# First blocks, moments and V weights reordered at the head of an attention kernel

## The chip, the core and the metric

The kernel runs on one core of a Trainium2 chip. The metric is the device time of one execution in microseconds (us). Before the change three runs gave 1567.88, 1568.05 and 1568.91, median 1568.05. One more execution was recorded by the profiler: it took 1567.75, of which the profile's span is 1566.0.

The engines are called as the profile calls them: PE is TensorE (PEld its weight loads), DVE VectorE, ACT ScalarE, POOL GpSimd, SP SyncE, which here only issues DMAs. "SPq", "ACTq" and "POOLq" are an engine's instructions that issue DMAs.

## The reference

```python
B, S, D, H, F = 1, 2048, 512, 32, 1376         # heads of 16
xn = (x - mean(x)) / sqrt(var(x) + 1e-5)        # over D
q, k, v = split(xn @ wqkv)                      # D x 3D
p = softmax(q @ k.T * 16 ** -0.5)               # per head, 2048 x 2048
s = (p @ v) @ wo
g = silu(gelu(xn @ w1 + b1) @ w2 + b2)          # D x F, F x D
out = x + s * g                                 # everything float32
```

## The kernel before

The 2048 tokens are 16 blocks (t) of 128 and 4 chunks (c) of 512, so a chunk is four blocks. Every large product of the first half is made of three matmuls on rounded halves: an operand is split in a high part (rounded to the matmul's type by a copy on ACT) and a low part (operand minus high part, on DVE or POOL), and the terms are high·high, low·high and high·low. `mm3` (L81) issues the three for one slice of the contraction.

The order of all instructions is written out by hand; each engine runs its own in that order and waits on semaphores for what it reads. DMAs stand in the queue of the engine that issues them, in the order of issue. Three parts follow each other: the root (to about 45 us), where xn, its transposes and the first q, k and V come about; the MLP with the remaining q and k and the maxima of the scores (to about 478 us); and the attention loop with the projection behind it. The change lies in the root alone.

The root, by its helpers:

- `load_x` (L402) loads a block of x, 256 KB. Blocks 1 and 3 are on ACT's queue, the others on SP's, in this order: x 0, x 2, the q and k weights of two groups, x 4 and 5, four pieces of V's weights (`wv_r`). Each further block takes the buffer of the one six before it (XB = 6), once that one's norm has read it.
- `moments` (L411, L412): bn_stats and bn_aggr of one block on DVE, into mv.
- `rstd` (L416 to L421) for four blocks at once: add eps (DVE), square root (ACT), reciprocal and three DVE steps that refine it (a Newton step). All are 128x4 elements.
- `norm` (L425): one 128x512 pass of DVE per block into xn; then the load of the block six later is issued.
- `ln(t, n)`: moments of n blocks, one rstd, n norms.
- `turn` (L434): four PE transposes of a block, then `split` of the result in xh and xl: high copy on ACT (L75), low part on DVE (L76).
- `pool_after` (L492): a one-element POOL operation that reads xn of a block, and so parks POOL until that block's norm is done.
- V's weights: high copies on ACT (L503), low parts on POOL (`wv_low`, L495), four pieces k each, in the space of a later kt tile (the profile calls them kt).
- the q and k weights of the first two groups: high on ACT (L289), low on POOL (L290).
- `q_first(c)` (L450): 24 matmuls for one chunk, three terms by two groups by four k. `evac` takes the result out: ACT copies both groups from PSUM (hg, L365), rounds both (hh, L369), POOL makes the low parts (hl, L370), and SP stores both to DRAM (qk_h L375, qk_l L376).
- `v_tile(t)` (L81): 12 matmuls of a V block, and `v_out`.
- `load_first`: after q_first(1), twelve gathers on SP's queue (L124 and L142) that read chunk 0's and chunk 1's q and k back from DRAM in another layout (gt), for the first score matmuls (L190).
- `consts`: on POOL, a memset, the DMA of ones, a cast of the identity, and the DMAs of b1 and b2.

PE's order in the root is: 22 dummy matmuls on the identity, transposes of blocks 0 to 3, q_first(0), transposes of 4 to 7, v_tile(0), q_first(1), transposes of 8 to 11, v_tile(1), q_first(2), transposes of 12 to 15, then the pairs of the MLP and the score part, where the first L190 read gt.

ACT's order is the square root of blocks 0 to 3, the weights' high copies, the four L75 of blocks 0 to 3, four L503, the square root of 4 to 7, hg and hh of chunk 0, the L75 of 4 to 7, and so on. POOL's is `pool_after(3)`, two L290, three L495, consts, `pool_after(7)`, the fourth L495, hl of chunk 0, and so on.

Of the kernel before, what the change touches and what calls it, by code (L numbers as in the profile page):

```python
# [8 lines left out]
F32 = mybir.dt.float32  # L9
F32R = mybir.dt.float32r  # L10
AF = mybir.ActivationFunctionType
# [5 lines left out]
P = 128  # L17
# [32 lines left out]
def fused(ctx: ExitStack, tc: tile.TileContext, x, wqk, wv, wo, w1, b1, w2, b2, out):  # L50
# [307 lines left out]

    def evac(us, ph):
        raws = [wk.tile([P, CH], F32, name="hg", bufs=2) for u in us]  # L360
        for u, raw in zip(us, raws):
            if u[0] == "m":
                nc.scalar.activation(raw, ph.pop(u), AF.Gelu_apprx_tanh, bias=b1_sb[:, u[2]:u[2] + 1])
            else:
                nc.scalar.activation(raw, ph.pop(u), AF.Copy)  # L365
        for u, raw in zip(us, raws):
            hh = wk.tile([P, CH], F32R, name="hh", bufs=HB)
# [16 lines left out]
    with ExitStack() as s1:  # L384
# [14 lines left out]
        def load_x(t):  # L399
            xs[t] = w1k.tile([P, D], F32, name="xt", bufs=XB)  # L400
            eng = nc.scalar if t in (1, 3) else nc.sync
            eng.dma_start(xs[t], x[t * P:(t + 1) * P, :])  # L402
# [3 lines left out]
        mv = wp.tile([P, NT, 2], F32, name="mv")  # L406
        ve = wp.tile([P, 5, NT], F32, name="ve")

        def moments(t):
            st = w1k.tile([P, 6], F32, name="st")  # L410
            nc.vector.bn_stats(st, xs[t])  # L411
            nc.vector.bn_aggr(mv[:, t, :], st)  # L412

        def rstd(t0, t1):
            v = ve[:, :, t0:t1]
            nc.vector.tensor_scalar(v[:, 0], mv[:, t0:t1, 1], EPS, None, op0=OP.add)  # L416
            nc.scalar.activation(v[:, 1], v[:, 0], AF.Sqrt)
            nc.vector.reciprocal(v[:, 2], v[:, 1])
            nc.vector.scalar_tensor_tensor(v[:, 3], v[:, 2], -0.5, v[:, 2], op0=OP.mult, op1=OP.mult)
            nc.vector.tensor_mul(v[:, 3], v[:, 3], v[:, 0])  # L420
            nc.vector.scalar_tensor_tensor(v[:, 4], v[:, 3], 1.5, v[:, 2], op0=OP.add, op1=OP.mult)  # L421

        def norm(t):
            xns[t] = w1k.tile([P, D], F32, name="xn", bufs=4)
            nc.vector.tensor_scalar(xns[t], xs.pop(t), mv[:, t, 0:1], ve[:, 4, t:t + 1],  # L425
                                    op0=OP.subtract, op1=OP.mult)
            if t + XB < NT:
                load_x(t + XB)
# [9 lines left out]
        def v_tile(t):  # L438
            pv = a_tile((P, D))
            c, ts = t // NCH, slice(t % NCH * P, t % NCH * P + P)  # L440
            for k in range(KT):
                mm3(pv, (xh[c][:, k, ts], xl[c][:, k, ts]), (wv_h[:, k], wv_l[:, k]), k == 0, k == KT - 1)
            v_out(t, pv)

        def q_first(c):
            pq = {("q", g, c): a_tile((P, CH)) for g in range(2)}
            for n, (i, j) in enumerate(((0, 0), (1, 0), (0, 1))):
                for g in range(2):
                    for k in range(KT):
                        nc.tensor.matmul(pq["q", g, c], W1[g][i][:, k * P:(k + 1) * P], (xh, xl)[j][c][:, k],  # L450
                                         start=n == 0 and k == 0, stop=n == 2 and k == KT - 1)
            evac(list(pq), pq)

        for t in range(4):
            load_x(t)
        warm = wp.tile([1, 2], F32, name="warm")
        nc.vector.memset(warm, 1.0)
        nc.scalar.activation(warm[:, 1:], warm[:, :1], AF.Sqrt)
        for g in range(2):
# [11 lines left out]
        def consts():  # L471
# [4 lines left out]
            nc.gpsimd.tensor_copy(ident_r, ident)  # L476
            nc.gpsimd.dma_start(b1_sb, b1)
            nc.gpsimd.dma_start(b2_sb, b2.rearrange("(o d) -> o d", o=1).to_broadcast([P, D]))

        pw = ps_v.tile([P, D], F32, name="pv")  # L480
        for _ in range(22):
            nc.tensor.matmul(pw[:, :P], ident, ident, start=True, stop=True)
        def ln(t, n):
            for i in range(t, t + n):
                moments(i)
            rstd(t, t + n)
            for i in range(t, t + n):
                norm(i)
# [9 lines left out]
        for g in range(2):  # L498
            W1[g] = w_split(W1[g], "w1", 4)
        for t in range(NCH):  # L500
            turn(t)
        for k in range(KT):
            nc.scalar.activation(wv_h[:, k], wv_r[:, k], AF.Copy)  # L503
        for k in range(KT - 1):
            wv_low(k)
        ln(NCH, NCH)
        consts()
        pool_after(2 * NCH - 1)
        wv_low(KT - 1)
        q_first(0)  # L510
        for c in range(1, NCH):
            for t in range(NCH * c, NCH * c + NCH):
                turn(t)
            if c < NCH - 1:
                ln(NCH * c + NCH, NCH)
            else:
                nc.scalar.activation(warm[:, 1:], warm[:, :1], AF.Gelu_apprx_tanh)
                w1_load(0)
                w2_load(0)
                w2_load(1)  # L520
                break
            v_tile(c - 1)
            q_first(c)
            if c == 1:
                load_first()

    keep_r = ctx.enter_context(tc.tile_pool(name="keep_r", bufs=1, side="right"))
# [521 lines left out]
```

## Time and profile before

| what | value |
|---|---|
| median of three runs | 1568.05 us |
| profiled execution | 1567.75 us |
| its span | 1566.0 us |
| PE busy | 1555.4 us (99%) |
| DVE busy | 1390.1 us (89%) |
| ACT busy | 1244.4 us (79%) |
| POOL busy | 375.4 us (24%) |
| PE busy, 0 to 9.73 / 9.73 to 19.45 / 19.45 to 42 us | 6.92 / 7.88 / 22.55 us |
| granted PE clock | 1.00 in every window |

Times in the profile run from the span's start. A line of a timeline has the start, the length from the first start to the last end of a group, the engine, the line of the kernel, the operation, what it writes and reads (partitions by elements), the count, and in brackets how long the engine had stood idle before and what ended that. Matmuls overlap, so the pitch of a row of them is taken from start to start. A line of the chain of waits has start, length and work; it is followed back from the last instruction of the window to what released each. A DMA's time from issue to landing is longer than its issue instruction.

### The profile page before, as it was taken

To read this page: it belongs to the slowest core of one execution; us is meant where nothing else is said; L and a number is where in the kernel's file an instruction comes from. 1 tells how busy PE (TensorE), PEld (TensorE's weight loads), DVE (VectorE), ACT (ScalarE), POOL (GpSimd) and SP (SyncE) were. 2 spreads that over 40 slices of the span, in tenths; PEclk is the share of its full clock that TensorE was granted. 3 is DMA by queue.
4 is the path that set the end of the run, shared out by engine and by line. 5 is a ranking of instruction groups with operands and counts; after the bars stand their busy time and mean duration, and the time that the engine had idled before them with its cause. 6 is when DMAs were issued, how large, how long until landed. Compare 5 with 4: busy or idle time off the path is not lost.

```text
span 1566.0 us, 32580 instructions
## 1 busy us (share of the span) xinstructions
PE 1555.4 (99%) x12254; PEld 955.0 (61%) x12254; DVE 1390.1 (89%) x2306; ACT 1244.4 (79%) x2487; POOL 375.4 (24%) x392
## 2 busy tenths in 40 slices
PE   8999999999999999999999999999999999999998
PEld 7899999999995444444444444444444444444455
DVE  7899999999998999999999999999999999999833
ACT  4333343434338999999999999999999999999994
POOL 4135574756752000000000100010110000000144
PEclk9999999999999999999999999999999999999999
DMA  6515443356435012311111311131141111110162
GB/s 217 159 47 139 116 156 108 112 148 152 140 89 117 21 42 43 60 30 30 43 29 28 65 30 43 43 73 36 36 73 30 33 29 30 43 30 22 45 209 104
DMA packets 79501, 117.38 MB, mean 75 GB/s; under 512 B 28876, under 2 KB 29132, under 8 KB 77968
## 3 DMA queue, kind: packets, MB, share of 16 engines
q1 hardware_dynamic: 75884, 102.36, 23.8%
q0 software_dynamic: 2976, 12.35, 4.4%
q8 instruction: 97, 1.59, 0.4%
q10 hardware_dynamic: 484, 0.60, 0.1%
q14 instruction: 60, 0.49, 0.1%
HBM read 84.81 MB, written 25.97 MB: 71 GB/s over the span
## 4 chain that ended last, share of the span: by engine, by line
PE 98%; DVE 1%; DMA 0%; issue 0%; POOL 0%; ACT 0%; DVEq 0%
PE pv L800 33%; PE pst L737 15%; PE ps L737 14%; PE ps L569 13%; PE ps L190 10%; PE pst L569 7%; PE pv L569 3%; PE ps L906 2%; PE ps L450 1%; PE ps L81 1%; PE pst L81 1%; DVE st L411 0%; DMA xt<-in_x 0%; PE pst L434 0%; DVE slot L76 0%; DVE xn L425 0%
## 5 line engine op out<-in xcount | busy, mean ns | idle before, releaser
L195 DVE TENSOR_REDUCE mx<-ps 128x2 f32<-128x512 f32 x2048 | 1297.3, 684 | 109.2 <-PE ps L190 29.1
L739 ACT ACTIVATE slot<-pst 128x512 f32<-128x512 f32 x1533 | 803.6, 604 | 2.9 <-PE ps L190 1.6
L800 PE MATMUL pv<-slot,vsb 128*17 128x512 f32 (+1 forms) x4096 | 539.2, 598 | 0.1
L190 PE MATMUL ps<-kt,slot 48*128 48x512 f32 x1350 | 382.7, 371 | 1.1 <-POOLq L227 1.1
L739 ACT ACTIVATE slot<-ps 128x512 f32<-128x512 f32 x515 | 307.9, 598 | 7.5 <-PE ps L737 4.7
L737 PE MATMUL pst<-qt,kt 50*128 50x512 f32 x1149 | 304.4, 405 | 0.0
L737 PEld LDWEIGHTS ps<-qt,kt 50*128 50x128 f32 x387 | 70.7, 183 | 323.8 <-ACT slot L739 322.9
L190 PEld LDWEIGHTS ps<-kt,slot 48*128 48x128 f32 x1350 | 223.1, 184 | 5.4 <-POOLq L227 1.4
L569 PE MATMUL ps<-slot,w1h 64*128 64x512 f32 x1104 | 222.3, 393 | 0.0
L737 PEld LDWEIGHTS pst<-qt,kt 50*128 50x128 f32 x1149 | 207.4, 184 | 21.3 <-DVE gt L654 1.2
L737 PE MATMUL ps<-qt,kt 50*128 50x512 f32 x387 | 190.9, 495 | 0.0
L190 PE MATMUL ps<-kt,qz 48*128 48x512 f32 x448 | 186.8, 417 | 0.0
L190 PE MATMUL ps<-slot,slot 48*128 48x512 f32 x584 | 168.5, 372 | 0.0
L569 PEld LDWEIGHTS ps<-slot,w1h 64*128 64x128 f32 x1104 | 156.0, 185 | 5.0 <-ACT junk L583 0.2
L569 PE MATMUL ps<-slot,w1l 64*128 64x512 f32 x552 | 145.3, 392 | 0.0
L370 POOL TENSOR_TENSOR hl<-hg,hh 128x512 fp32r<-128x512 f32 x76 | 96.9, 1297 | 134.6 <-ACT hh L369 94.4
L800 PEld LDWEIGHTS pv<-slot,vsb 128*17 128x17 f32 (+1 forms) x4096 | 68.8, 96 | 83.7 <-issue 31.6
L583 ACT ACTIVATE junk<-ident_r 1x1 f32<-1x1 f32 x94 | 18.4, 196 | 126.3 <-PE pst L569 118.2
L737 PE MATMUL pst<-qt,slot 50*128 50x512 f32 x384 | 99.6, 405 | 0.0
L190 PEld LDWEIGHTS ps<-slot,slot 48*128 48x128 f32 x584 | 97.1, 184 | 3.3 <-DVE mx L195 1.2
L837 POOL TENSOR_TENSOR slot<-slot,dn 64x512 f32<-64x512 f32 x16 | 20.5, 1281 | 312.4 <-PE pst L737 167.3
L190 PEld LDWEIGHTS ps<-kt,qz 48*128 48x128 f32 x448 | 82.0, 183 | 15.4 <-DVE mx L195 0.8
(153 smaller groups left out, 1764.2 us busy)
## 6 DMA issues: line engine op xcount, KB each, us to landing
raw<-in_w SPq DMA_DIRECT2D x88, 256.0 KB
qk_h<-hh SPq DMA_DIRECT2D x32, 256.0 KB
qk_l<-hl SPq DMA_DIRECT2D x32, 256.0 KB
qt<-qk_h SPq DMA_DIRECT2D x128, 64.0 KB
slot<-qk_h SPq DMA_DIRECT2D x92, 64.0 KB
g_d<-gt POOLq DMA_DIRECT2D x16, 256.0 KB, 3.0
qt<-qk_l SPq DMA_DIRECT2D x64, 64.0 KB
kt<-qk_h POOLq DMA_DIRECT2D x16, 256.0 KB, 6.4
```

The lines of the kernel that those rows point to most:

```text
L81: nc.tensor.matmul(ps, lhs[a], rhs[b], start=first and n == 0, stop=last and n == 2)
L190: return nc.tensor.matmul(ps[:, c0:c0 + w], QS[u][r, p, qi * P:(qi + 1) * P], keys, start=True, stop=True).ins
L195: nc.vector.tensor_reduce(MX[u][:, 2 * p:2 * p + 2, qi, ki][:, heads, parts], ps.rearrange("p (n c) -> p n c", c=HC), axis=AX.X, op=OP.max)
L370: nc.gpsimd.tensor_sub(hl, raw, hh.bitcast(F32))
L450: nc.tensor.matmul(pq["q", g, c], W1[g][i][:, k * P:(k + 1) * P], (xh, xl)[j][c][:, k], start=n == 0 and k == 0, stop=n == 2 and k == KT - 1)
L569: i = nc.tensor.matmul(ps, lhs[r], rhs[r], start=first, stop=last).ins
L583: i = nc.scalar.activation(junk[:, :1], ident_r[:1, :1].bitcast(F32), AF.Copy).ins
L737: nc.tensor.matmul(ps, kts[KSET[g]][p][r, k * P:(k + 1) * P], QT[u][r, p, :], start=True, stop=True)
L739: nc.scalar.activation(PT[u, k][:, 2 * p + a, :], ps, AF.Exp, scale=SCALE)
L800: nc.tensor.matmul(PV[u][32 * j:32 * j + w, :], vsb[:, k, h:h + w], PT[u, k][:, j, :], start=(k == 0), stop=(k == NT - 1))
L837: eng.tensor_mul(ot[c][rs, g // 2], ot[c][rs, g // 2], DN.pop(u)[rs])
L906: op = nc.tensor.matmul(PW[b][0], OTS[b, k][i][r], (wo_h, wo_l)[j][r, k], start=part == 0 and n == 0, stop=part == 3 and n == 5).ins
```

## The change

It has seven parts, all in the root; PE's order of matmul groups is the same.

1. Blocks 0 and 1 stand on SP's queue, 2 and 3 on ACT's. The DMA of b1 moves from POOL to the head of ACT's queue.
2. rstd has five steps: eps is the bias of the square root, and the add for the Newton step is folded into one of its operations. ve has four rows instead of five; a tile eps is set by a memset.
3. `act_moments`: the mean and the variance of block 7 are made on ACT, by a copy with a sum, a square with a sum, and a small copy. The passes' full results go to the tile that later takes xn of block 7.
4. The first term of q_first(0) is made in two halves of 256 columns, so 16 matmuls of 128x256 in place of 8 of 128x512; the first half reads tokens of blocks 0 and 1 alone.
5. V's high copy and low part of k = 0 stay early. The high copies of k = 1 to 3 move behind the square root of blocks 4 to 7 on ACT, the low parts behind `pool_after(7)` on POOL. v_tile runs its terms one after the other over all k, that with the low weights last.
6. `evac` takes a function that is called between the hg and the hh copies: the transposes and splits of the next chunk. On ACT the next chunk's four L75 stand between hg and hh, for chunks 0, 1 and 2.
7. `consts` is called after q_first(0).

```diff
@@ -356,13 +356,15 @@
     wv_h, wv_l = [kv[:, i].rearrange("p (k d) -> p k d", d=D) for i in range(2)]
     hl_of = {}
 
-    def evac(us, ph):
+    def evac(us, ph, then=None):
         raws = [wk.tile([P, CH], F32, name="hg", bufs=2) for u in us]
         for u, raw in zip(us, raws):
             if u[0] == "m":
                 nc.scalar.activation(raw, ph.pop(u), AF.Gelu_apprx_tanh, bias=b1_sb[:, u[2]:u[2] + 1])
             else:
                 nc.scalar.activation(raw, ph.pop(u), AF.Copy)
+        if then:
+            then()
         for u, raw in zip(us, raws):
             hh = wk.tile([P, CH], F32R, name="hh", bufs=HB)
             hl = wk.tile([P, CH], F32R, name="hl", bufs=HB)
@@ -398,31 +400,39 @@
 
         def load_x(t):
             xs[t] = w1k.tile([P, D], F32, name="xt", bufs=XB)
-            eng = nc.scalar if t in (1, 3) else nc.sync
+            eng = nc.scalar if t in (2, 3) else nc.sync
             eng.dma_start(xs[t], x[t * P:(t + 1) * P, :])
 
         ident = wp.tile([P, P], F32, name="ident")
         wv_r = wp.tile([P, KT, D], F32, name="wv_r")
         mv = wp.tile([P, NT, 2], F32, name="mv")
-        ve = wp.tile([P, 5, NT], F32, name="ve")
+        ve = wp.tile([P, 4, NT], F32, name="ve")
+        eps = wp.tile([P, 1], F32, name="eps")
 
         def moments(t):
             st = w1k.tile([P, 6], F32, name="st")
             nc.vector.bn_stats(st, xs[t])
             nc.vector.bn_aggr(mv[:, t, :], st)
 
+        def act_moments(t):
+            sq = xns[t] = w1k.tile([P, D], F32, name="xn", bufs=4)
+            acc = w1k.tile([P, 1], F32, name="acc")
+            nc.scalar.activation(sq, xs[t], AF.Copy, scale=1.0 / D, accum_out=mv[:, t, 0:1])
+            nc.scalar.activation(sq, xs[t], AF.Square, bias=mv[:, t, 0:1], scale=-1.0, accum_out=acc)
+            nc.scalar.activation(mv[:, t, 1:2], acc, AF.Copy, scale=1.0 / D)
+
         def rstd(t0, t1):
-            v = ve[:, :, t0:t1]
-            nc.vector.tensor_scalar(v[:, 0], mv[:, t0:t1, 1], EPS, None, op0=OP.add)
-            nc.scalar.activation(v[:, 1], v[:, 0], AF.Sqrt)
-            nc.vector.reciprocal(v[:, 2], v[:, 1])
-            nc.vector.scalar_tensor_tensor(v[:, 3], v[:, 2], -0.5, v[:, 2], op0=OP.mult, op1=OP.mult)
-            nc.vector.tensor_mul(v[:, 3], v[:, 3], v[:, 0])
-            nc.vector.scalar_tensor_tensor(v[:, 4], v[:, 3], 1.5, v[:, 2], op0=OP.add, op1=OP.mult)
+            v, var = ve[:, :, t0:t1], mv[:, t0:t1, 1]
+            nc.scalar.activation(v[:, 0], var, AF.Sqrt, bias=eps)
+            nc.vector.reciprocal(v[:, 1], v[:, 0])
+            nc.vector.scalar_tensor_tensor(v[:, 2], v[:, 1], -0.5, v[:, 1], op0=OP.mult, op1=OP.mult)
+            nc.vector.scalar_tensor_tensor(v[:, 2], var, EPS, v[:, 2], op0=OP.add, op1=OP.mult)
+            nc.vector.scalar_tensor_tensor(v[:, 3], v[:, 2], 1.5, v[:, 1], op0=OP.add, op1=OP.mult)
 
         def norm(t):
-            xns[t] = w1k.tile([P, D], F32, name="xn", bufs=4)
-            nc.vector.tensor_scalar(xns[t], xs.pop(t), mv[:, t, 0:1], ve[:, 4, t:t + 1],
+            if t not in xns:
+                xns[t] = w1k.tile([P, D], F32, name="xn", bufs=4)
+            nc.vector.tensor_scalar(xns[t], xs.pop(t), mv[:, t, 0:1], ve[:, 3, t:t + 1],
                                     op0=OP.subtract, op1=OP.mult)
             if t + XB < NT:
                 load_x(t + XB)
@@ -438,23 +448,34 @@
         def v_tile(t):
             pv = a_tile((P, D))
             c, ts = t // NCH, slice(t % NCH * P, t % NCH * P + P)
-            for k in range(KT):
-                mm3(pv, (xh[c][:, k, ts], xl[c][:, k, ts]), (wv_h[:, k], wv_l[:, k]), k == 0, k == KT - 1)
+            for n, (i, j) in enumerate(((0, 0), (1, 0), (0, 1))):
+                for k in range(KT):
+                    nc.tensor.matmul(pv, (xh, xl)[i][c][:, k, ts], (wv_h, wv_l)[j][:, k],
+                                     start=n == 0 and k == 0, stop=n == 2 and k == KT - 1)
             v_out(t, pv)
+
+        def turns(c):
+            for t in range(NCH * c, NCH * c + NCH):
+                turn(t)
 
         def q_first(c):
             pq = {("q", g, c): a_tile((P, CH)) for g in range(2)}
             for n, (i, j) in enumerate(((0, 0), (1, 0), (0, 1))):
-                for g in range(2):
-                    for k in range(KT):
-                        nc.tensor.matmul(pq["q", g, c], W1[g][i][:, k * P:(k + 1) * P], (xh, xl)[j][c][:, k],
-                                         start=n == 0 and k == 0, stop=n == 2 and k == KT - 1)
-            evac(list(pq), pq)
-
+                m = 2 if n == c == 0 else 1
+                for cs in (slice(h * CH // m, (h + 1) * CH // m) for h in range(m)):
+                    for g in range(2):
+                        for k in range(KT):
+                            nc.tensor.matmul(pq["q", g, c][:, cs], W1[g][i][:, k * P:(k + 1) * P],
+                                             (xh, xl)[j][c][:, k, cs], start=n == 0 and k == 0 and cs.start == 0,
+                                             stop=n == 2 and k == KT - 1)
+            evac(list(pq), pq, lambda: turns(c + 1))
+
+        nc.scalar.dma_start(b1_sb, b1)
         for t in range(4):
             load_x(t)
         warm = wp.tile([1, 2], F32, name="warm")
         nc.vector.memset(warm, 1.0)
+        nc.vector.memset(eps, EPS)
         nc.scalar.activation(warm[:, 1:], warm[:, :1], AF.Sqrt)
         for g in range(2):
             W1[g] = w_new(wqk[:, g], 2, "raw1")
@@ -474,15 +495,15 @@
             nc.gpsimd.dma_start(ones_d.rearrange("r (n c) -> r n c", c=P // 2),
                                 one.to_broadcast([2, 2 * NT, P // 2]))
             nc.gpsimd.tensor_copy(ident_r, ident)
-            nc.gpsimd.dma_start(b1_sb, b1)
             nc.gpsimd.dma_start(b2_sb, b2.rearrange("(o d) -> o d", o=1).to_broadcast([P, D]))
 
         pw = ps_v.tile([P, D], F32, name="pv")
         for _ in range(22):
             nc.tensor.matmul(pw[:, :P], ident, ident, start=True, stop=True)
-        def ln(t, n):
+        def ln(t, n, given=()):
             for i in range(t, t + n):
-                moments(i)
+                if i not in given:
+                    moments(i)
             rstd(t, t + n)
             for i in range(t, t + n):
                 norm(i)
@@ -497,32 +518,32 @@
         pool_after(NCH - 1)
         for g in range(2):
             W1[g] = w_split(W1[g], "w1", 4)
-        for t in range(NCH):
-            turn(t)
-        for k in range(KT):
+        turns(0)
+
+        def wv_high(k):
             nc.scalar.activation(wv_h[:, k], wv_r[:, k], AF.Copy)
-        for k in range(KT - 1):
+
+        wv_high(0)
+        wv_low(0)
+        act_moments(2 * NCH - 1)
+        ln(NCH, NCH, (2 * NCH - 1,))
+        for k in range(1, KT):
+            wv_high(k)
+        pool_after(2 * NCH - 1)
+        for k in range(1, KT):
             wv_low(k)
-        ln(NCH, NCH)
+        q_first(0)
         consts()
-        pool_after(2 * NCH - 1)
-        wv_low(KT - 1)
-        q_first(0)
-        for c in range(1, NCH):
-            for t in range(NCH * c, NCH * c + NCH):
-                turn(t)
-            if c < NCH - 1:
-                ln(NCH * c + NCH, NCH)
-            else:
-                nc.scalar.activation(warm[:, 1:], warm[:, :1], AF.Gelu_apprx_tanh)
-                w1_load(0)
-                w2_load(0)
-                w2_load(1)
-                break
+        for c in range(1, NCH - 1):
+            ln(NCH * c + NCH, NCH)
             v_tile(c - 1)
             q_first(c)
             if c == 1:
                 load_first()
+        nc.scalar.activation(warm[:, 1:], warm[:, :1], AF.Gelu_apprx_tanh)
+        w1_load(0)
+        w2_load(0)
+        w2_load(1)
 
     keep_r = ctx.enter_context(tc.tile_pool(name="keep_r", bufs=1, side="right"))
     qring = ctx.enter_context(tc.tile_pool(name="qring", bufs=2, side="right"))
```

## The prediction

> **What bounds the kernel now.** I read first the page's busy shares, then the table by windows to see where TensorE idles, then the chain of waits from 0 to 20 us, the DMA view of the first 15 us, and the timelines of each engine around the changed lines.
>
> ```profile
> span 1566.0 us, 32580 instructions
> PE 1555.4 (99%) x12254; PEld 955.0 (61%) x12254; DVE 1390.1 (89%) x2306; ACT 1244.4 (79%) x2487; POOL 375.4 (24%) x392
> 9.73:19.45 9.72, 7.88 (x40) 6.14 (x41) 9.12 (x22) 5.84 (x12) 7.93 (x10) 1.00 0.47 156
> 19.45:42.00 22.55, 22.55 (x122) 18.71 (x124) 17.89 (x45) 10.77 (x23) 8.22 (x9) 1.00 0.75 207
> 42.00:100.00 58.00, 58.00 (x492) 52.81 (x492) 52.13 (x83) 17.04 (x37) 11.95 (x12) 1.00 0.38 109
> 300.00:1550.00 1250.00, 1248.78 (x9818) 677.06 (x9816) 1116.74 (x1842) 1128.22 (x2234) 219.40 (x249) 1.00 0.25 61
> ```
> In a windows line stand the window, its length, then the busy time of PE, PEld, DVE, ACT, POOL, the granted clock, DMA share and GB/s. From 19.45 us on TensorE has no gap to 100 us, and 1.2 us of idle time in the 1250 us after 300; the clock is 1.00. So the program is a packed TensorE stream behind a root of 19.45 us, and the change touches the root and the 25 us behind it. The time can move only by how much earlier or later the stream stands once the edits are passed. Before 19.45 VectorE is the busy one (9.12 of 9.72).
>
> ```profile
> 0.76 3.78 DMA xt<-in_x
> 7.89 0.18 DVE ve L416
> 8.09 0.21 ACT ve L417
> 16.78 0.92 DVE ve L416
> 17.72 0.21 ACT ve L417
> 18.76 0.56 DVE xn L425
> 19.45 1.08 PE L434 MATMUL ps<-ident,xn 128*128 128x128 f32 x8 [1.05 <-DVE xn L425]
> ```
> The chain (start, length, work) is the arrival of block 0, the moments of blocks 0 to 3, rstd, norm, splits, the same for blocks 4 to 7, and the transposes of block 4, for which TensorE waited 1.05 us. I call this point T1 (19.45) and the norm of block 4 N (18.76).
>
> **Gains ahead of T1.**
>
> *Front.* Block 0 gets the SP queue's first place and block 1 stands behind it; b1 (44 bytes a row) leads the ACT queue, then blocks 2 and 3.
>
> ```profile
> GB/s 0 0 0 0 38 169 186 300 213 393 393 410 388 393 339 300 399 306 219 322 382 410 399 415 393 404 410 393 279 197 371 377 421 197 289 290 360 246 109 76
> 4.56 0.69 DVE L411 BATCH_NORM_STATS2 st<-xt 128x6 f32<-128x512 f32 x1 [3.69 <-DMA xt<-in_x]
> 5.39 0.66 DVE L411 BATCH_NORM_STATS2 st<-xt 128x6 f32<-128x512 f32 x1
> 15.07 0.66 DVE L411 BATCH_NORM_STATS2 st<-xt 128x6 f32<-128x512 f32 x1
> 15.87 0.66 DVE L411 BATCH_NORM_STATS2 st<-xt 128x6 f32<-128x512 f32 x1
> 16.78 0.91 DVE L416 TENSOR_SCALAR ve<-mv 128x4 f32<-128x4 f32 x1
> 13.84 3.81 POOL L495 TENSOR_TENSOR kt<-wv_r,kt 128x512 fp32r<-128x512 f32 x3
> ```
> Each GB/s figure is a slice of 0.375 us. By 4.56 some 0.79 MB had moved, three blocks' worth (0.26 MB each), when block 0 came. Sharing with one other block instead, it is complete at 0.52 MB, about 3.65: at best 0.9 gained. But the four blocks then still come out of one pool of engines, and VectorE needs the second one 0.8 later (the pitch from 15.07 to 15.87). Block 1, queued behind block 0, may land as late as the third did: VectorE took that one 1.6 us behind the first, which is 0.8 too late. The term is thus +0.9 to -0.8; I take +0.40, nearer the byte count.
>
> [...]
>
> *rstd.* One step of six goes: the add of eps. Its place was 7.89 to 8.09, so 0.20 at blocks 0 to 3. At blocks 4 to 7 it was 16.78 to 17.72: 0.94, since the step took 0.91 and ended right after GpSimd's L495 did (13.84 + 3.81 = 17.65). In the new order GpSimd has three fewer L495 there and ScalarE reads the variance itself; 0.94 goes.
>
> *Block 7's moments* leave VectorE: one pitch, 0.80. On ScalarE they are two 128x512 passes and a small one.
>
> ```profile
> 12.36 2.21 ACT L503 ACTIVATE kt<-wv_r 128x512 fp32r<-128x512 f32 x4
> 11.40 1.09 ACT L75 ACTIVATE slot<-pst 128x512 fp32r<-128x512 f32 x2
> 12.55 1.19 PE L450 MATMUL pst<-slot,w1h 128*128 128x512 f32 x4 [0.79 <-ACT slot L75]
> 24.15 1.10 PE L450 MATMUL ps<-slot,w1h 128*128 128x512 f32 x4
> 1555.15 0.39 PE L81 MATMUL pst<-kt,oh 128*128 128x256 f32 x2
> 1555.51 0.63 PE L81 MATMUL ps<-kt,oh 128*128 128x512 f32 x2
> 21.31 3.01 PE L81 MATMUL pst<-kt,slot 128*128 128x512 f32 x12
> ```
> A pass takes 0.55 (2.21 for four), a small one 0.21: 1.3. Three of the four copies of V's high halves move behind the square root, so ScalarE is free from about 12.9. Block 7 (its load waits for block 1's norm, which itself comes 0.60 earlier) precedes blocks 8 and 9 on its queue; counting 0.52 MB back from the end of the GB/s row puts it at 12.75. The square root is wanted at 17.72 - 2.34 = 15.38, so the moments end 1.3 ahead. That cover hides them; if the block comes 1.3 later than I count, each further tenth is on the path, at most 0.80 in all. I take 0.
>
> *Halves of columns.* The first q term waited 0.79 for the copies of blocks 2 and 3. With halves it starts after two copies. Sixteen 256-column matmuls at 0.12 (1555.15 to 1555.51 for three) cost 1.92, eight full ones at 0.237 (21.31 to 24.15 for twelve) 1.90: no price. Nor a gain in itself, since TensorE idles before T1; but T1 moves up by 2.34 and the front and rstd carry q by only 0.60, so of the 1.05 idle nothing would remain and 0.69 would be lost; the 0.75 of the halves gives it back, with 0.06 to spare. The Newton steps use fewer rows of ve, and eps is a memset ahead of everything: 0.
>
> Sum ahead of T1: 0.40 + 0.20 + 0.80 + 0.94 = 2.34.
>
> **Losses behind T1.**
>
> *V's low halves.* Three of four now stand behind the tiny GpSimd op that waits for block 7's norm, where one stood.
>
> ```profile
> 21.01 1.27 POOL L495 TENSOR_TENSOR kt<-wv_r,kt 128x512 fp32r<-128x512 f32 x1
> 22.26 2.54 POOL L370 TENSOR_TENSOR hl<-hg,hh 128x512 fp32r<-128x512 f32 x2
> 30.01 0.60 ACT L365 ACTIVATE hg<-ps 128x512 f32<-128x512 f32 x1 [0.32 <-PE ps L450]
> 30.50 1.14 ACT L369 ACTIVATE hh<-hg 128x512 fp32r<-128x512 f32 x2
> 31.54 0.59 ACT L75 ACTIVATE slot<-ps 128x512 fp32r<-128x512 f32 x1
> 32.02 1.57 ACT L75 ACTIVATE slot<-pst 128x512 fp32r<-128x512 f32 x3
> 33.79 0.32 SPq L376 DMA_DIRECT2D qk_l<-hl  x1
> 39.38 0.30 SPq L142 DMA_DIRECT2D gt<-qk_l  x1
> 41.14 0.42 SPq L142 DMA_DIRECT2D gt<-qk_h  x1
> g_d<-gt POOLq DMA_DIRECT2D x16, 256.0 KB, 3.0
> 45.61 0.40 PE L190 MATMUL ps<-gt 48*128 48x512 f32 x1
> ```
> Against N they start at 21.01 - 18.76 = 2.25 and end at 2.25 + 3.81 = 6.06. The new order of terms puts the low weights last; the V tile's twelfth matmul starts at 24.15 - 0.24 - 18.76 = 5.15. TensorE waits 0.91 (0 if the copies run faster alone, but 1.27 apiece alone and in threes speaks for 0.91). Queued behind on GpSimd are hl of chunk 0, then the memset, the ones and b2 DMAs and the cast (17.61 to 20.5 in the old order, a stretch of about 3) and hl of chunk 1; only the last is near a user, and it comes 6 us later.
>
> The same pieces can meet VectorE. [...] It would cost rstd of blocks 8 to 11 up to 1.3, whose turn at TensorE is 6 us later; 0 in the sum.
>
> *The split evacuation.* The transposes of the next chunk stand between hg and hh, so on ScalarE four L75 (0.49 apiece) go ahead of the two hh: hh, hl and both stores of chunk 1 leave 1.95 later against TensorE. Everything of the first gather stands behind them on SP: the store of qk_l issued at 33.79 held the gather until 39.38, and the last gather was issued at 41.14. Its reader ran at 45.61 without waiting. How long it had lain there no row says: with 3.0 from issue to landing (the g_d row) 1.47, with the 5.59 of the store before it, none. I take 0.4, nearer the store, as it is the same queue in the same stretch. Stall: 1.95 - 0.4 = 1.55, between 0.48 and 1.95. Past it every reader sits later in a packed stream, and further loads have what this stall gave them.
>
> Before chunk 1 the same reordering brings L75 forward by 1.1 and costs nothing.
>
> **Sum.** 2.34 - 0.91 - 1.55 = -0.12. The profiled execution took 1567.75 (1566.0 of span and 1.75 around it), 0.30 under the median of 1568.05; carried to the median: 1568.2. The difference that a measurement of this kernel can tell from none is about 0.2%, 3.1 us.
>
> **Rivals.**
>
> *A, the gather had room.* If its slack was above 1.95 there is no second stall: 2.34 - 0.91 = 1.43 gained, 1566.6. For: the reader never waited. Against: SP issues to the end of the chain, store by store.
>
> *B, both losses hidden.* Then V's pieces also finish in time, and the whole 2.34 stands: 1565.7. For: GpSimd is only 24% busy. Against: 6.06 against 5.15 comes from three rows that agree.
>
> *C, slower: block 1 is late.* Both of VectorE's first blocks share one queue; if block 1 lands 1.6 behind block 0 instead of 0.8 or less, VectorE stands idle between them and the front is -0.8. This decides from 5.39 us on: a second stats later than that is a loss. Then 2.34 - 1.2 = 1.14 gained, 2.46 lost, +1.32: 1569.4.
>
> [...]
>
> **How the numbers follow.** Forecast 0.44, with 1567.2 to 1569.0 by the gather's 0.48 to 1.95 and the front's rest; A 0.15, B 0.14, C 0.11, D 0.04; 0.12 for what I have not seen, in a chain that passes through five engines. From 1565.6 to 1569.6 holds all five with the ends of their costs. No case reaches 3.1 us: the largest gain, front at 0.9 and no loss, is 2.84. Only the unseen goes past: faster 0.07, slower 0.05, same 0.88.
>
> **What would show it.** Right: first stats at about 4.15, the second at most 0.85 later; block 4's norm at about 16.4; no L416 of 0.9; a gap of TensorE of 0.9 in the V tile, released by GpSimd's L516; one of about 1.5 at the second L190, released by a load. The stream at 45.6 then stands where it stood. Wrong: no gap at L190 (A), none at both (B), a wait of VectorE between its first two stats (C), or any gap past 60 us, which this sum does not have.

## The result, and the profile after

The changed kernel takes 1570.90 us (median of 15 runs, 1569.99 to 1573.30) where the kernel before takes 1567.91 (15 runs, 1567.72 to 1568.91). The ratio is 1.0021, with a 95% interval from 1.0014 to 1.0028: slower by 3.0 us, where 1568.2 was forecast and the range ended at 1569.6. The profiled execution took 1571.81, that is 4.06 more than the profiled one of before, and 0.9 over the median. It is one of four of the fifteen with a mean granted clock of 0.998; these took 1571.81 to 1572.68, and of the eleven others only one was as slow (1573.30).

The page's first lines and four lines of the table by windows, changed kernel:

```profile
span 1569.9 us, 32599 instructions
PE 1558.4 (99%) x12262; PEld 959.0 (61%) x12262; DVE 1389.1 (88%) x2301; ACT 1246.2 (79%) x2492; POOL 374.1 (24%) x391
```
```profile
9.73:19.45 9.72, 9.13 (x49) 8.30 (x50) 8.96 (x22) 7.02 (x16) 3.92 (x4) 0.82 0.48 161
19.45:42.00 22.55, 22.31 (x123) 18.50 (x121) 17.24 (x42) 11.61 (x24) 10.97 (x12) 1.00 0.72 194
42.00:100.00 58.00, 56.14 (x463) 50.32 (x465) 48.52 (x77) 14.79 (x32) 10.52 (x10) 1.00 0.46 114
300.00:1550.00 1250.00, 1248.76 (x9831) 678.51 (x9828) 1119.82 (x1845) 1128.03 (x2236) 219.52 (x249) 1.00 0.24 60
```

Three things differ from before: the granted clock is 0.82 ahead of 19.45, TensorE idles 0.24 behind it, and between 42 and 100 us, where it had no gap, it has 1.86 us of them. From there on the two kernels run alike. The matmul counts of the third window say more than its idle time, since matmuls of 64 rows often start in pairs there (two at 42.09 in the kernel before, of 0.39 each), and TensorE counts as busy with one of a pair missing (one alone at 46.54 and one at 46.77 in the changed kernel, with no idle time between): 463 in place of the 492 of before, 29 fewer, are 3.4 us at 58 us for 492.

**The root.** VectorE's timeline, first the four stats of blocks 0 to 3, then the norms of blocks 4 to 7; below it TensorE's and the windows around the first q term:

```profile
3.54 0.69 DVE L414 BATCH_NORM_STATS2 st<-xt 128x6 f32<-128x512 f32 x1 [2.63 <-DMA xt<-in_x]
4.85 0.70 DVE L414 BATCH_NORM_STATS2 st<-xt 128x6 f32<-128x512 f32 x1 [0.40 <-DMA xt<-in_x]
5.68 0.66 DVE L414 BATCH_NORM_STATS2 st<-xt 128x6 f32<-128x512 f32 x1
7.64 0.69 DVE L414 BATCH_NORM_STATS2 st<-xt 128x6 f32<-128x512 f32 x1 [1.08 <-DMA xt<-in_x]
17.95 1.92 DVE L435 TENSOR_SCALAR xn<-xt,mv,ve 128x512 f32<-128x512 f32 x4
```
```profile
10.32 1.11 PE L444 MATMUL ps<-ident,xn 128*128 128x128 f32 x8 [2.19 <-DVE xn L435]
19.34 1.03 PE L444 MATMUL ps<-ident,xn 128*128 128x128 f32 x8
24.02 0.50 PE L453 MATMUL pst<-kt,slot 128*128 128x512 f32 x1 [0.24 <-POOL kt L516]
24.35 2.03 PE L468 MATMUL ps<-slot,w1h 128*128 128x512 f32 x8
```
```profile
11.00:12.00 1.00, 1.00 (x9) 0.96 (x8) 0.99 (x3) 0.98 (x2) 0.20 (x2) 0.78 0.82 158
12.00:13.00 1.00, 1.00 (x7) 1.00 (x6) 1.00 (x3) 0.71 (x3) 1.00 (x1) 0.50 1.01 385
13.00:14.00 1.00, 1.00 (x6) 1.00 (x6) 0.92 (x2) 1.00 (x2) 1.00 (x2) 0.50 0.97 295
14.00:15.00 1.00, 1.00 (x7) 1.00 (x6) 0.96 (x3) 0.97 (x4) 1.00 (x2) 0.52 0.65 250
```

Block 0's stats come 1.0 us earlier than before, blocks 1 and 2 0.5 earlier, and block 3's late: they start at 7.64 after 1.08 of idle time, where those of before started at 6.98. All four are needed, so the front lost 0.66. The norms of blocks 4 to 7 still start 0.81 earlier (17.95 against 18.76). But TensorE, which had idled 2.19 us ahead of the first transposes where it idled 1.43 before, then ran at half clock from about 11.5 to 15, and its q terms ended only at 19.34, where the transposes of block 4 followed without a gap. So T1 moved by 0.11 of the 2.34 that were forecast. The V tile's last matmul then waited for L516, the last low part of V, and stood at 24.02.

The gap of 2.19 belongs to this execution and not to the kernel alone. The same 22 dummies ended at 8.14 here and at 9.45 in the trace without part 6: by windows of 1 us their pace rises here from 6 to 8 matmul records to 11 or 12, at about 5 us; there, by an estimate from these paces and the end at 9.45, it does so at about 7.5. The clock column reads 1.00 from 0 to 9.73 in both. With the same order of loads the runs without part 6, with V's pieces early and with the weights behind the kt loads idled 0.65, 1.58 and 1.17 there and kept the full clock (1.00 from 9.73 to 19.45); where V's pieces stood as in the change, T1 was then 18.24 and 17.97, so 1.2 to 1.5 of the 2.34 came.

**Behind it.** The chain of waits that ends at the second reader of kt, its longer pieces in order of time:

```profile
35.94 5.78 DMA qk_l<-hl
41.74 0.30 SPq L142
42.09 1.64 SPq L142
43.77 2.00 DMA gt<-qk_h
45.77 0.24 PE ps L190
46.64 0.41 SPq L378
47.10 0.60 SPq L284
47.75 6.01 DMA raw<-in_w
53.78 6.71 DMA kt<-qk_l
60.59 0.47 PE ps L190
```

Read down: the store of chunk 1's qk_l, issued at 35.94 (33.79 before); the gathers that had waited for it; the first L190; the stores of chunk 2 behind the gathers on SP's queue; the MLP's first weights behind those; and behind them the kt loads, the last of which was issued at 53.78. Its like was issued at 49.93 before (SyncE's timeline of before):

```profile
49.93 0.30 SPq L110 DMA_DIRECT2D kt<-qk_l  x1
```

The readers of gt and of kt, TensorE's timeline, in the kernel before and in the changed one, and the first L800 of each, which is L821 in the changed kernel (before's second reader of gt, at 45.61, stands in the prediction):

```profile
44.86 0.44 PE L190 MATMUL ps<-gt 48*128 48x512 f32 x1
56.23 0.44 PE L190 MATMUL ps<-kt,gt 48*128 48x512 f32 x1
57.05 0.41 PE L190 MATMUL ps<-kt,gt 48*128 48x512 f32 x1
478.89 1.06 PE L800 MATMUL pv<-slot,vsb 128*32 128x512 f32 x8
```
```profile
45.76 0.47 PE L190 MATMUL ps<-gt 48*128 48x512 f32 x1 [0.59 <-DMA gt<-qk_h]
47.17 0.47 PE L190 MATMUL ps<-gt 48*128 48x512 f32 x1
58.81 0.47 PE L190 MATMUL ps<-kt,gt 48*128 48x512 f32 x1 [0.88 <-DMA kt<-qk_l]
60.59 0.47 PE L190 MATMUL ps<-kt,gt 48*128 48x512 f32 x1 [0.38 <-DMA kt<-qk_l]
482.78 1.06 PE L821 MATMUL pv<-slot,vsb 128*32 128x512 f32 x8
```

Against before, the stream stands 0.20 late at q_first(1) (24.35 against 24.15), 0.90 at the first L190 (45.76 against 44.86), 1.56 at the second, 2.58 and 3.54 at the first two readers of kt, and 3.89 at 478.89. Most of the loss, then, arose between 44 and 61 us.

### The profile page after: what moved, and what is told of

It is laid out like the page before. It is cut to its first block, busy times and chain, and to the rows that moved or that the text cites. A ratio compares the mean times of both kernels' runs of the same rounds, so it can differ in the third digit from the quotient of the medians.

```text
span 1569.9 us, 32599 instructions
## 1 busy us (share of the span) xinstructions
PE 1558.4 (99%) x12262; PEld 959.0 (61%) x12262; DVE 1389.1 (88%) x2301; ACT 1246.2 (79%) x2492; POOL 374.1 (24%) x391
## 4 chain that ended last, share of the span: by engine, by line
PE 96%; DMA 2%; DVE 0%; POOL 0%; ACT 0%; issue 0%; SPq 0%; ACTq 0%
PE pv L821 32%; PE pst L758 15%; PE ps L758 14%; PE ps L590 13%; PE ps L190 10%; PE pst L590 7%; PE pv L590 2%; PE ps L927 1%; PE ps L468 1%; PE ps L81 0%; DMA kt<-qk_l 0%; PE pst L81 0%; DMA raw<-in_w 0%; DMA xt<-in_x 0%; DMA qk_l<-hl 0%
## 5 line engine op out<-in xcount | busy, mean ns | idle before, releaser
L821 PE MATMUL pv<-slot,vsb 128*17 128x512 f32 (+1 forms) x4096 | 539.3, 599 | 0.2 <-DVE os L828 0.2
L190 PE MATMUL ps<-kt,slot 48*128 48x512 f32 x1350 | 383.1, 372 | 1.1 <-POOLq L227 1.1
L190 PEld LDWEIGHTS ps<-kt,slot 48*128 48x128 f32 x1350 | 223.5, 184 | 5.8 <-POOLq L227 1.4
L190 PE MATMUL ps<-kt,qz 48*128 48x512 f32 x448 | 187.5, 419 | 0.0
L190 PE MATMUL ps<-slot,slot 48*128 48x512 f32 x584 | 168.7, 372 | 0.0
L821 PEld LDWEIGHTS pv<-slot,vsb 128*17 128x17 f32 (+1 forms) x4096 | 69.0, 96 | 83.1 <-issue 29.6
L190 PEld LDWEIGHTS ps<-slot,slot 48*128 48x128 f32 x584 | 97.3, 184 | 3.5 <-DVE mx L195 1.2
L190 PEld LDWEIGHTS ps<-kt,qz 48*128 48x128 f32 x448 | 82.1, 183 | 16.2 <-DVE mx L195 1.0
```

Of the source, the lines that this page charges most:

```text
L190: return nc.tensor.matmul(ps[:, c0:c0 + w], QS[u][r, p, qi * P:(qi + 1) * P], keys, start=True, stop=True).ins
L821: nc.tensor.matmul(PV[u][32 * j:32 * j + w, :], vsb[:, k, h:h + w], PT[u, k][:, j, :], start=(k == 0), stop=(k == NT - 1))
```

## The experiments

Theory S: the split evacuation (part 6) sends the stores of chunk 1 off late, and gathers, chunk 2's stores and kt loads follow on SP's queue. Rivals: R, the root costs it; V, the V tile's wait.

| kernel | median, us | before on that chip | ratio, 95% interval |
|---|---|---|---|
| changed | 1570.90 | 1567.91 | 1.0021, 1.0014 to 1.0028 |
| without part 6 | 1567.41 | 1567.63 | 1.0002, 0.9993 to 1.0011 |
| without part 1 | 1569.79 | 1567.63 | 1.0014, 1.0005 to 1.0023 |
| V's pieces early | 1570.05 | 1567.63 | 1.0017, 1.0008 to 1.0026 |
| before + part 6 | 1569.78 | 1567.63 | 1.0013, 1.0004 to 1.0022 |
| before + part 6, chunk 1 only | 1570.15 | 1567.72 | 1.0017, 1.0008 to 1.0026 |
| before + part 6, chunk 2 only | 1568.12 | 1567.72 | 1.0003, 0.9994 to 1.0011 |
| recombined | 1566.22 | 1567.72 | 0.9991, 0.9982 to 1.0000 |
| recombined, x on one queue | 1567.08 | 1567.72 | 0.9998, 0.9989 to 1.0007 |
| recombined, weights behind k | 1566.07 | 1567.91 | 0.9989, 0.9980 to 0.9998 |
| changed, weights behind k | 1568.54 | 1567.91 | 1.0003, 0.9994 to 1.0011 |
| before, weights behind k | 1567.77 | 1567.91 | 1.0000, 0.9991 to 1.0009 |
| changed, 44 dummies | 1575.39 | 1567.91 | 1.0047, 1.0035 to 1.0060 |
| changed, 31 dummies | 1571.81 | 1567.86 | 1.0025, 1.0016 to 1.0034 |
| before + part 1 | 1568.20 | 1567.86 | 1.0003, 0.9994 to 1.0012 |

**Without part 6.**

```diff
-            evac(list(pq), pq, lambda: turns(c + 1))
+            evac(list(pq), pq)
+            turns(c + 1)
```


> The changed kernel with part 6 alone undone: hg and hh stand together again, and the next chunk's transposes follow. Theory S (the stores of chunks 1 and 2 leave late and everything behind them on SP's queue comes late, 0.95 us of stalls at the first L190 and 2.05 at the kt readers in the profile after): those stalls go, the time falls by 2.5 to 3.5 to 1567.5 to 1568.5, TensorE idle between 42 and 100 us under 0.3. Rival R (the root costs it: block 3 lands at 7.62 and the clock is halved for 3.4 us): the time stays at 1570 to 1571. Rival V (the V tile's wait on the low weights): stays too.

1567.41, 0.22 under before's median: against before, the 3.0 that the change lost are gone and 0.2 more, 0.1 beyond the range that S named. Theory S holds against R and V. Its window from 42 to 100 us, and its V tile:

```profile
42.00:100.00 58.00, 57.86 (x484) 51.98 (x484) 51.47 (x81) 16.40 (x36) 10.93 (x11) 1.00 0.43 109
```
```profile
23.59 0.50 PE L453 MATMUL pst<-kt,slot 128*128 128x512 f32 x1 [0.73 <-POOL kt L517]
```
0.14 of idle time is left of 1.86. By the counts (484 matmuls against 492 and 463) about 0.9 of 3.4 us is still lost in this execution, which at 1568.15 ran 0.7 over its median; the last kt load was issued at 51.79, and the chain to its reader runs through the weights (raw, 45.78 to 51.77) and no longer through the gathers. The V tile's wait is longer than in the changed kernel, since TensorE came sooner: eleven matmuls from 19.99 at 0.237 would have put the twelfth at 22.6, and it started at 23.59: 0.99.

**Without part 1, and with V's pieces early.**

```diff
-            eng = nc.scalar if t in (2, 3) else nc.sync
+            eng = nc.scalar if t in (1, 3) else nc.sync
-        nc.scalar.dma_start(b1_sb, b1)
+            nc.gpsimd.dma_start(b1_sb, b1)                 # in consts
```


> The changed kernel with part 1 alone undone: blocks 1 and 3 on ACT's queue, b1 on POOL's. Theory S: the stalls behind 42 us stay, so 1569.5 to 1570.5, at most 1.0 faster than the changed kernel from the norm of block 0, which comes 0.6 to 0.8 earlier, and from a clock that stays at 1.00. Rival R: all of the loss goes, 1567 to 1568. The fourth stats start at about 7.0 in place of 7.64 under both.

1569.79: the queues' places cost about 0.8 by the medians (2.99 over before became 2.16; the two intervals overlap), and the rest stayed, as S said. The fourth stats start at 6.91.

```diff
-        wv_high(0)
-        wv_low(0)
+        for k in range(KT):
+            wv_high(k)
+        for k in range(KT - 1):
+            wv_low(k)
...
-        for k in range(1, KT):
-            wv_low(k)
+        wv_low(KT - 1)
```


> The changed kernel with part 5's moves undone (high copies of V's weights early, three of four low parts early; the order of the terms stays new). Theory S: the V tile's wait of 0.4 goes, the later stalls take most of it back: 1570.0 to 1570.9. Rival V: 1568 or less.

1570.05, within S's bounds. Its timeline shows what the early pieces do. One Newton step of VectorE, of the usual 0.16 us, takes 0.85 and ends as GpSimd's L516 does (14.64 + 3.80 = 18.44):

```profile
17.62 0.85 DVE L428 SCALAR_TENSOR_TENSOR ve<-ve 128x4 f32<-128x4 f32 x1
14.64 3.80 POOL L516 TENSOR_TENSOR kt<-wv_r,kt 128x512 fp32r<-128x512 f32 x3
```
So the stall that stood at L416 before was not removed with L416; it went with the two of three early pieces of GpSimd that part 5 moved away, as the prediction had it but for their number.

**Part 6 alone, then chunk by chunk.** The kernel before with `evac(us, ph, then)` as in the change, for all chunks, for chunk 1 alone, and for chunk 2 alone:

```diff
-            evac(list(pq), pq)
+            evac(list(pq), pq, (lambda: turns(c + 1)) if c == 1 else None)
+            if not (c == 1):
+                turns(c + 1)
```


> The kernel before with part 6 alone. Theory S: stalls at the first L190 and at the kt readers, 2 to 3.5 us slower than before: 1570 to 1571.4. Rivals R and V: like before, 1567.5 to 1568.5.

> The kernel before with the split evacuation for chunk 1 alone. Theory S1 (the gathers hang on chunk 1's stores, they hold SP's queue, and the stores of chunk 2 and the kt loads follow them): nearly all of what the split cost on its own, +1.5 to +2.2, so 1569.1 to 1569.9. Rival S2 (the kt readers hang on chunk 2's own later stores): +0.5 to +0.9 from the gathers alone, 1568.1 to 1568.6.

> The kernel before with the split evacuation for chunk 2 alone. Theory S1: hh of chunk 2 is 2 us later, but SP is held by the gathers until 41.6 anyway; 0 to +0.6, 1567.6 to 1568.3. Rival S2: +1.3 or more, 1568.9 or later, with idle time at the kt readers and none at the first L190.

Over before they cost 2.15, 2.43 and 0.40. The first time lies 0.22 under what S named, the second 0.25 over what S1 named. As far as the intervals tell, chunk 1 alone makes the whole of it; chunk 2's 0.40 cannot be told from none. Chunk 1's first kt reader, and ScalarE's and SyncE's timelines of chunk 2's evacuation in that kernel:

```profile
57.73 0.47 PE L190 MATMUL ps<-kt,gt 48*128 48x512 f32 x1 [0.83 <-DMA kt<-qk_l]
40.31 1.14 ACT L371 ACTIVATE hh<-hg 128x512 fp32r<-128x512 f32 x2
44.15 0.37 SPq L377 DMA_DIRECT2D qk_h<-hh  x1
```
Chunk 2's evacuation has its old order in that kernel, and its hh were ready at 41.45; the first store went at 44.15, right behind the last gather (issued at 43.63, for 0.42). So it is the gathers ahead of them on the queue that hold its stores. S1 holds, S2 falls.

**The weights behind the kt loads.** The four loads of the MLP's first weights (1 MB) go behind the kt loads on SP's queue, in the changed kernel and, as a control, in the kernel before:

```diff
-        w1_load(0)
-        w2_load(0)
-        w2_load(1)
...
     load_k(0, c0=CH, n=S - 2 * CH)
+    w1_load(0)
+    w2_load(0)
+    w2_load(1)
```


> The changed kernel with the same one edit. Theory Q: of the 2.05 lost at the kt readers 1 to 2 come back, the 0.9 at the first L190 stays: 1.0007 to 1.0014 of before. Rival: unchanged at 1.0019 to 1.0021.

> The kernel before with the same one edit, as a control. It shows no wait at its kt readers, so under Theory Q nothing is there to be won: 0.9997 to 1.0003 of before. A gain here would say that the edit helps in some other way than by that wait.

The changed kernel falls to 1568.54, the kernel before does not move (1567.77). In the first the readers of kt no longer wait; the gathers' readers still do:

```profile
46.06 0.47 PE L190 MATMUL ps<-gt 48*128 48x512 f32 x1 [0.41 <-issue]
56.50 0.45 PE L190 MATMUL ps<-kt,gt 48*128 48x512 f32 x1
57.34 0.40 PE L190 MATMUL ps<-kt,gt 48*128 48x512 f32 x1
```
More came back than expected (2.4 by the two medians over before, against 1 to 2): so the kt loads had been late by the weights as well as by the stores' delay. In the traces the stream falls back by 3.34 from q_first(1) to the second kt reader in the changed kernel, and by 0.76 here. Whether the weights held the loads by their place in the queue or by their share of the transfers, these runs do not tell.

**Recombined.** Parts 2, 3, 4 and the order of V's terms, old queues, no split, and two pieces of V early instead of one (the edit for V's pieces; the others as above):

```diff
-        wv_high(0)
-        wv_low(0)
+        for k in range(2):
+            wv_high(k)
+            wv_low(k)
...
-        for k in range(1, KT):
-            wv_low(k)
+        for k in range(2, KT):
+            wv_low(k)
```


> The changed kernel without parts 1 and 6, and with two of V's four pieces early (high copy and low part of k = 0 and 1) in place of one. Two pieces end on GpSimd at about 16.3, before the Newton steps of blocks 4 to 7, so that these stay at 0.17 apiece; the other two end before the V tile's last matmul. Expected: norm of block 4 at 17.0, no gap in the V tile, q_first(1) 1.8 earlier than before, and the time 1.4 to 2.0 under before, 1565.6 to 1566.2. If instead the gathers and kt loads set the pace by themselves, what is won at 23 us is lost at 45 and 57, and it stays at 1567 to 1567.6.

1566.22, 1.5 under before, as expected, with an interval that just reaches 1. The norm of block 4, the V tile without a gap, and q_first(1), VectorE's and TensorE's timeline:

```profile
16.84 1.92 DVE L435 TENSOR_SCALAR xn<-xt,mv,ve 128x512 f32<-128x512 f32 x4
19.29 3.01 PE L453 MATMUL pst<-kt,slot 128*128 128x512 f32 x12
22.14 2.02 PE L468 MATMUL ps<-slot,w1h 128*128 128x512 f32 x8
```
q_first(1) starts 2.01 earlier than before (22.14 against 24.15). 0.6 of it was lost again at the first kt reader (54.79 against 56.23). With the weights behind the kt loads:

> The recombined kernel with the four loads of the MLP's first weights issued behind the kt loads on SP's queue, not ahead of them; their first reader comes at about 69 us. Theory Q (at 54 us TensorE waits for kt loads that stand behind 1 MB of weights on the queue): the wait of 0.65 goes and the 2.0 gained at 24 us stay, 0.4 to 0.8 under the recombined kernel, 0.9985 to 0.9988 of before. Rival (the kt loads wait for the stores' landing alone, wherever the weights stand): no change, 0.9990.

```profile
42.00:100.00 58.00, 58.00 (x492) 52.78 (x488) 52.26 (x83) 16.07 (x35) 10.81 (x11) 1.00 0.40 108
```
No idle time is left there, and the time is 1566.07, 1.84 under before: 0.9989, with an interval that excludes 1. This version lies under both kernels, by 0.1% or little more. Its 0.34 over the recombined one, each against its own chip's before, is just under what was expected and lies within the two intervals; that the wait is gone is shown, the size of it is not.

**The front.** With blocks 0 to 3 all on SP's queue ahead of the weights (edit: every block's `dma_start` on `nc.sync`, on top of the recombined kernel):

> As the recombined kernel, and blocks 0 to 3 all on SP's queue ahead of the q and k weights, in order. If a queue serves its transfers in order and the queues share the engines, block 0 lands at 3.5 and block 3 before 5.9, so that VectorE runs its four stats without a wait and the norm of block 0 comes 0.9 earlier than with two queues: 0.6 to 1.0 faster than the recombined kernel. If the later arrival of the q and k weights takes its place: no gain or a loss of up to 0.5.

0.9 slower than the recombined kernel by the medians, where 0.6 to 1.0 faster was hoped for and at most 0.5 slower was the rival. Blocks 0 to 2 came in order as hoped, block 3 late again, though nothing but those three stood ahead of it (the stats of blocks 0, 2 and 3):

```profile
3.57 0.69 DVE L413 BATCH_NORM_STATS2 st<-xt 128x6 f32<-128x512 f32 x1 [2.66 <-DMA xt<-in_x]
5.26 0.69 DVE L413 BATCH_NORM_STATS2 st<-xt 128x6 f32<-128x512 f32 x1
7.23 0.69 DVE L413 BATCH_NORM_STATS2 st<-xt 128x6 f32<-128x512 f32 x1 [1.06 <-DMA xt<-in_x]
```
So neither b1 (back on POOL's queue here) nor weights ahead of it on its queue make block 3 late; what does, stays open. Nor is all of this run's loss the front's: of the 1.22 by which T1 is later than in the recombined trace (18.75 against 17.53), the norm of block 0 has 0.52. The rest is block 7, for whose load ScalarE waited until 15.08 there (13.80 was the start of its moments in the recombined trace), so that the moments ended at 16.89 and the square root had to wait for them. The kernel before with part 1 alone:

```diff
-            eng = nc.scalar if t in (1, 3) else nc.sync
+            eng = nc.scalar if t in (2, 3) else nc.sync
+        nc.scalar.dma_start(b1_sb, b1)                     # ahead of the loads of x
-            nc.gpsimd.dma_start(b1_sb, b1)                 # in consts
```


> The kernel before with part 1 alone (blocks 0 and 1 on SP's queue, b1 and blocks 2 and 3 on ACT's). Theory F (block 3 lands at 7.2 to 7.8 instead of 6.05, and VectorE, idle before it, starts the norms 0.4 to 0.9 later): 0.3 to 1.0 slower than before, 1.0002 to 1.0007, a little more where the clock falls. If the front pays as the prediction had it: 0.4 faster.

1568.20, 0.34 over before, within F's bounds, though the interval holds 1. Its profiled execution (1570.61) was its slowest, and it shows a longer gap and a longer stretch at half clock than the changed kernel's (9.72 x 0.35 / 0.5 = 6.8 us, by the window below):

```profile
10.53 1.48 PE L434 MATMUL ps<-ident,xn 128*128 128x128 f32 x8 [2.60 <-DVE xn L425]
```
```profile
9.73:19.45 9.72, 8.23 (x31) 6.77 (x32) 8.74 (x20) 5.07 (x10) 6.84 (x8) 0.65 0.46 161
```

**The clock.** More warm-up matmuls in the changed kernel (22 to 44, then to 31), to fill TensorE's idle time:

> The changed kernel with 44 warm-up matmuls in place of 22, which leave out nothing and add about 1.3 us of TensorE work before the first transposes. Theory C (the idle time of 2.2 us between the dummies and the late norm of block 0 lets the granted clock fall to one half for 3.4 us in some executions): the clock stays at 1.00 from 9 to 16 us, the slow executions (1571.3 and above) go, and the median falls by 0.3 to 1.0, to 1.0014 to 1.0018 of before. If the halving has another cause: still half in some, 1.0020 or more.

> The changed kernel with 31 warm-up matmuls. Forty-four ended at 12.27 us and held the first transposes up by 2 us; at their pace of 0.19 apiece 31 end at about 9.9, just ahead of the norm of block 0 at 10.3. Theory C (idle time of 2.2 us before the first transposes lets the granted clock fall to one half in some executions): the clock stays at 1.00 from 9 to 16 us, no execution has a mean clock of 0.998, and the median falls by 0.3 to 1.0, to 1.0012 to 1.0017 of before. Otherwise 1.0019 or more, with half-clock stretches left.

Forty-four were a mistake of size: they ended at 14.06 (1.37 + 12.69, and not at 12.27, as the expectation for 31 has it), held the transposes up to 13.90, and cost 4.5. With 31 the profiled execution has no idle time there and no stretch at half clock (1.00 from 9.73 to 19.45):

```profile
18.17 1.08 PE L444 MATMUL ps<-ident,xn 128*128 128x128 f32 x8 [0.38 <-DVE xn L435]
```
T1 stands at 18.17 and q_first(1) at 23.89, with the first transposes 0.28 earlier than in the changed kernel's trace (10.04 against 10.32). So by an estimate from these two traces the half clock put T1 back by 0.9 (19.34 - 18.17 - 0.28) but q_first(1) by only 0.2 (24.35 - 23.89 - 0.28), as the V tile waits for L516 either way. This execution took 1569.64 and was the fastest of its eleven; the median did not fall (1571.81), executions reached 1573.86, and two had a mean clock of 0.998. Theory C's expectation failed as to the median. What slows those executions no trace here shows, so the price of the half clock in the median stays open.

## Why the prediction was wrong

Two steps failed. The larger was the sentence that loads behind the gathers "have what this stall gave them": it priced the kt loads at nothing, and they lost about 2.0 us. The other was the front, taken at +0.40 and measured at about -0.8 by the medians. The items follow the prediction.

- What bounds the kernel, a packed stream that moves as a whole: right. The windows behind 100 us are alike in all traces (TensorE busy for all of 100 to 300 and for 1248.74 to 1248.78 of the 1250 us after it).
- Front, +0.40: wrong in sign, -0.66 in the profile, and about 0.8 by the run without part 1. The step that failed took the byte count for the order of arrival. (The GB/s row reaches 0.52 MB at 3.83 and not at 3.65, so the count itself gave 0.7; block 0's stats started at 3.54.) It weighed block 1's place (rival C's mechanism) and not block 3's. Rival C's size was right and its place wrong: block 1 was late by 0.40, block 3 by 1.08.
- rstd and L416: right in kind. The recombined trace has the norm of block 4 8.05 behind that of block 0 (16.84 - 8.79), where before had 9.63; 1.58 of the 1.74 forecast. Of the three early L495 one stayed and two moved, where the prediction counted three fewer. Two sizes were off: the square root with a bias took 0.30 and not 0.21, and block 7's moments on ScalarE took 1.8 (14.00 to 15.79) and not 1.3, for each sum is read out by an instruction of 0.19. The cover of 1.3 shrank to 1.0 and held; with all four blocks on one queue it did not.
- Halves of columns, no price and 0.06 to spare: not seen in the changed kernel, whose clock fell. In the recombined trace the sixteen halves took 2.03 (11.23 to 13.26) and eight full ones 1.86, a price of 0.17, and TensorE still idled 0.38 ahead of T1 (17.53). Without halves, by an estimate with the 2.82 and 5.85 that before took from the first transposes to the first q matmul and on to the end of q, q would have ended at 9.40 + 8.67 = 18.07. So they seem to have paid their way, as forecast; no run leaves them out.
- The clock was taken as 1.00 throughout from the windows of before, and in the profiled execution this was the step by which T1 lost what was left: behind 2.19 us of idle time it fell to 0.50. In the fifteen other traces of this study the idle time was 1.58 or less in fourteen, and their clock reads 1.00 from 9.73 to 19.45; it was 2.60 in the fifteenth, and that one reads 0.65. The half-clock stretch of the changed kernel lasts 3.4 (0.22/0.5 of a us in the window from 11 to 12, two full ones, 0.96 of the next). Whether the idle time brings it on, and what length of it is enough, no run shows.
- V's low halves, 0.91: right. They ended 6.01 behind the norm (forecast 6.06), and the wait was 0.99 without part 6; in the changed kernel 0.4, since the halved clock had made TensorE late as well.
- The split evacuation: the delay of 1.95 was exact (qk_l issued 2.15 later, with the stream 0.20 late), and the stall at the gathers' readers, 0.7 at the first and 1.4 with the second, was near the 1.55. The sentence that followed was the one that decided: "further loads have what this stall gave them" priced the kt loads at nothing. They lost a further 2.0 us (1.56 at the second gather reader, 3.54 at the second kt reader). Two gathers took 2.10 to issue in place of 0.90, chunk 2's stores stood behind them, and 1 MB of weights stood between them and the kt loads; the last kt load was issued 3.85 later, while the stream had been put back by only 1.56. The stall lent the kt loads no time that counted, since the queue that made it put them back by more.
- The range and the chances: D's 0.04 stood for a front that gives nothing since no block comes earlier; no run shows that, and block 0's stats came 1.0 earlier (3.54 against 4.56) with block 3's 0.66 later. By its own terms (front -0.8, V 0.91, gather 1.95) the slow end lay at 1569.8 and not at 1569.6, and the fast end at 1565.2 and not at 1565.6; the measured 1570.90 lies beyond either slow end. 0.05 stood for slower by over 0.2%, by "the unseen". Two of the prediction's own terms had the wrong sign or no price, and no rival joined them. With the front at -0.8 and the kt loads at 2.0 the sum would have been -3.3, near the measured -3.0.

## What to carry to other kernels

SP's queue issued its DMAs in the kernel's order here, and a store that went off 2.15 later (35.94 against 33.79) was followed by a last kt load that was issued 3.85 later (53.78 against 49.93), with its reader at 60.59: follow the queue to its end before a stall is called the last. Part 6 brought ScalarE's L75 of the next chunk forward and put the stores behind them back (1.95 for chunk 1's qk_l, measured against the stream), and here the stores were the critical ones. Judge an early arrival by the last block that the step needs, not by the first: block 0's stats came 1.0 earlier, block 3's 0.66 later, and the front lost 0.66.

## What the runs showed of the hardware

Block 3's stats started 1.35 to 2.2 us behind block 2's in every trace with another order of the first four loads than the old one (two on each of two queues in turn), where the pitch of VectorE's own work is 0.8 (5.39 to 6.18 to 6.98 in the kernel before); with one queue for all four as well. With those orders the slowest execution ran 1.2 to 2.6 us over the median (0.45 with 44 dummies), with the old one 0.3 to 1.7. The two ranges overlap. And half a clock was granted for 3.4 us behind an idle time of 2.19, and for 6.8 behind one of 2.60; behind 1.58 or less, in fourteen traces, the clock read 1.00 from 9.73 to 19.45.
